# Attention with one key block of six, and the last head's last, multiplied with v in 4-byte operands

## The chip, the cores and the metric

One core of one Trainium2 chip. The metric is the device time of one execution in microseconds: 743.06 us, the median of 3 runs (742.97 to 743.62).

## What is computed

Attention over 4 batches of 8 heads, 768 positions and 64 columns, in which a query sees only keys whose 6 sign bits of a random projection are the same, and behind it a layer of 8 experts. The change touches the attention alone:

```python
q_bits = (np.einsum('bhsd,dk->bhsk', q, proj) > 0); k_bits = ...
mask = q_bucket[:, :, :, None] == k_bucket[:, :, None, :]
scores = np.where(mask, scale * np.matmul(q, k.transpose(0, 1, 3, 2)), -1e9)
scores = scores - np.max(scores, axis=-1, keepdims=True)
attn = np.exp(scores)
attn = attn / (np.sum(attn, axis=-1, keepdims=True) + 1e-09)
return np.matmul(attn, v)
```

The result of attention decides which tokens each expert takes, in order of their logits.

## The kernel before

The work is one program on five engines, whose order is written out by hand. Attention (`attention`, up to about 405 us) takes the 32 heads one after the other, in 8 groups G of 4 heads. A head has 768 keys, which are 6 key blocks `kc` of 128.

A number of 4 bytes is kept as two numbers of 2 bytes, a high part and a low part, and a product is made of products of parts. For v these are `VH` (f16, with a 65th column of ones that gives the row sums) and `VL`, made for each head by `cv` (L186, a cast on ACT) and `sv` (L187, a subtraction).

The loop at the end of `attention` runs over steps t, one key block each, and in a step over the letters of `ORD`, 'SF0r1LRA':

- S: `S_pass` (L230, L232): scores of 128 queries on PE, and DVE's maximum over keys.
- 0 and 1: `ST` (L254 to L256): the transposed scores of block t, 384 queries at a time, in two matmuls on PE, and the exponential on ACT into `pt`, 128 keys by 768 queries of 4 bytes.
- L: `lo` (L259): the low part of `pt`, that is `pt` less its own upper two bytes read as bf16, for the block of the step before. `PAT` gives blocks 0 and 5 of even heads and block 3 of odd ones to DVE, and the rest to POOL; the first two heads have lists of their own, and the last block of all is DVE's.
- F or A: `AV` (L269 to L271): the product of block t-4 (`LAG` is 4) with v, accumulated in PSUM (`psv`). For each of the 6 pieces of 128 queries there are three matmuls, with 128 weight columns of `pt` or `lo` and 64 or 65 moving columns of v:

```python
T.matmul(av[:,c,:],ph[:,r],VH[u][:,j,kc,:],...)
T.matmul(av[:,c,0:64],ph[:,r],VL[u][:,j,kc,:],...)
T.matmul(av[:,c,:],l[:,r],VH[u][:,j,kc,:],...)
```

- r and R: everything with a step number of its own: the casts and subtractions for the next groups, `project` (L142, signs of a later group: 4-byte operands, 32 weight columns, 384 moving ones), `m_rows` (L239, L240), `sumv` (L197 to L200), and after each pair of heads `xtr` (L296 to L298, 4-byte transposes of 128 by 128).

After the last block `norm` divides by the row sums. Behind attention the routing and the 8 experts follow (from L312 on); the change does not touch them.

Of the kernel before, what the change touches and what calls it, by code (L numbers as in the profile page):

```python
# [8 lines left out]
F32 = mybir.dt.float32  # L9
F16 = mybir.dt.float16  # L10
# [3 lines left out]
ALU = mybir.AluOpType  # L14
# [4 lines left out]
AP=dict(PAT=[[0, 5], [3]],  # L19
 ORD='SF0r1LRA',  # L20
 LAG=4,
 E0=[3, 5],
 E1=[3, 4],
 X=[2, 2, 5],
 MR=2,
 LEAD=9,
 S=[7, 30],
# [3 lines left out]
 P3=[69, 73, 82, 80, 84, 86, 89, 86, 75, 83, 87, 90, 94, 96, 97, 99, 2, 3, 115, 58, 62, 87],  # L31
 P4=[-33, -33, -25, -21, -13, -7, -11, -7, -20, -16, -5, -2, -7, 5, 8, 3, 1, 4, 14, -56, -51, -11],
 L0=[89, 4],
 EA=[268, 32, 5],
 MV=[23, 24, 28, 59, 96, 1],
 CL=9,
# [3 lines left out]
PAT,E0,E1,DW,LEAD=(AP[k] for k in ('PAT','E0','E1','DW','LEAD'))  # L40
# [3 lines left out]
def attention(tc, nc, ctx, qT, kT, vv, proj, wg, x_dram, L, jp, identf, B, late=None, after=None):  # L44
    S=768; NG=2*B; NH=8*B; LAG=AP['LAG']
    cp=ctx.enter_context(tc.tile_pool(name="cp",bufs=1))
    dp=ctx.enter_context(tc.tile_pool(name="dp",bufs=2))
# [3 lines left out]
    V=nc.vector; A=nc.scalar; G_=nc.gpsimd; T=nc.tensor; SY=nc.sync  # L51
    BOTH=slice(0,2)

    LD={}
    def alloc_load(G):
        LD[G]=(dp.tile([128,2,S],F32,name="qp",bufs=1),dp.tile([128,2,S],F32,name="kp",bufs=1),dp.tile([128,4,6,64],F32,name="vp",bufs=1))
# [32 lines left out]
    pos=row(96,1.0,"pos"); neg=row(99,-1.0,"neg")  # L89
    kc=cp.tile([128,1],F32,name="kc"); V.scalar_tensor_tensor(kc,c70,-6.0,pos,op0=ALU.mult,op1=ALU.add)  # L90
    V.tensor_tensor(kc,kc,neg,op=ALU.add)
    QA=[];KA=[];QB=[];KB=[];VH=[];VL=[];WF=[]
    for u in range(2):
        for l,n in ((QA,"qa"),(KA,"ka"),(QB,"qb"),(KB,"kb")): l.append(cp.tile([128,4,2*HK if l is KA else S],F16,name=f"{n}{u}"))
    def init(j,eng):
# [18 lines left out]
    for u in range(2):  # L114
        VH.append(cp.tile([128,4,6,65],F16,name=f"vh{u}")); VL.append(cp.tile([128,4,6,64],F16,name=f"vl{u}"))
        G_.memset(VH[u][:,:,:,64:65],1.0)
        WF.append(cp.tile([128,4,65],F16,name=f"wf{u}")); G_.memset(WF[u],0.0)


# [28 lines left out]
    def sides(G):  # L148

        return [(slice(64*hh,64*hh+64),2+hh) for hh in range(2)]  # L150
    def his(G):
        u=G%2; h=TMP[G,'h']
        for qk,(a,b,r0) in enumerate(((QA,QB,0),(KA,KB,64))):
            for r,j in sides(G): SY.dma_start(a[u][0:64,j,0:S],h[qk][r,1])
            for r,j in sides(G): SY.dma_start(b[u][r0:r0+64,j,:],h[qk][r,1])
    def dbits(G):
        u=G%2; bt=TMP[G,'b']
        for hh in range(2):
            for w,dst in enumerate((QA,KA)): SY.dma_start(dst[u][64:70,2+hh,0:S],bt[64+32*w+6*hh:70+32*w+6*hh,:])
    def lows(G):  # L160
        u=G%2; l=TMP[G,'l']
        for r,j in sides(G): SY.dma_start(KB[u][0:64,j,:],l[1][r,1]); SY.dma_start(QB[u][64:128,j,:],l[0][r,1])
    def moves(G,part=0):


        u=G%2; h=TMP[G,'h']; l=TMP[G,'l']; bt=TMP[G,'b']
        hs=[(slice(64*hh,64*hh+64),slice(hh,4,2)) for hh in range(2)]
        def go(dst,src,r0=0):
            for r,js in hs: SY.dma_start(dst[u][r0:r0+64,js,0:S],src[r])
        def signs_():  # L170
            for j in range(4):
                for w,dst in enumerate((QA,KA)):
                    a=64*(j//2)+32*w+6*(j%2)
                    SY.dma_start(dst[u][64:70,j,0:S],bt[a:a+6,:])
        def nxt(w):
            if G+1<NG: load(G+1,w)
        if part==1: todo=(go,QA,h[0]),(go,KA,h[1]),(signs_,)
        elif part==2: todo=(go,QB,h[0]),(nxt,0),(go,KB,h[1],64),(nxt,1)
        elif part==3: todo=()
        else: todo=(go,QA,h[0]),(go,QB,h[0]),(nxt,0),(go,KA,h[1]),(go,KB,h[1],64),(signs_,),(nxt,1)  # L180
        for f,*x in todo: f(*x)
        if part in (0,3): go(KB,l[1]); go(QB,l[0],64)
    def clear(G):

        SY.dma_start(QA[G%2][96:128].rearrange("p j (z q) -> p (j z) q",z=2),wrm[0:32,None,0:384].to_broadcast([32,8,384]))
    def cv(G,j): A.copy(VH[G%2][:,j,:,0:64],LD[G][2][:,j])  # L186
    def sv(G,j,e=None): (e or V).tensor_tensor(VL[G%2][:,j],LD[G][2][:,j],VH[G%2][:,j,:,0:64],op=ALU.subtract)  # L187
    def sumv(G):
        u=G%2
        if G<2:  # L190
            V.tensor_copy(WF[u][96:128,:,64],wc[96:128,:].to_broadcast([32,4]))
        ps=psT.tile([128,512],F32,name="pst")
        pv=ps[96:128,0:256].rearrange("p (j d) -> p j d",j=4)
        n=0
        for c in range(6):
            for src in (VH[u],VL[u]):
                T.matmul(ps[:,0:256].rearrange("p (j d) -> p j d",j=4),on,src[:,:,c,0:64],start=n==0,stop=n==11,skip_group_check=True); n+=1  # L197
        hi=dp.tile([128,4,64],F16,name="shi",bufs=1)
        A.copy(hi[96:128],pv)
        V.scalar_tensor_tensor(WF[u][96:128,:,0:64],hi[96:128],ml[96:128],pv,op0=ALU.mult,op1=ALU.add)  # L200
# [20 lines left out]
        else: G_.tensor_tensor(QB[0][64:128,j],qd[64:128,j],QB[0][64:128,j],op=ALU.subtract)  # L221


    M6={}
    def S_pass(h,qc):
        G,j=divmod(h,4); u=G%2
        if qc==0: M6[h]=dp.tile([128,6],F16,name="m6",bufs=3)
        ps=psS.tile([128,2,512],F32,name="pss")
        for hf in range(2):
            T.matmul(ps[:,hf,0:HK],QA[u][:,j,qc*128:qc*128+128],KA[u][:,j,hf*HK:hf*HK+HK],start=True,stop=True)  # L230
            if h==0: warm(DW[1],DW[4])
        V.tensor_reduce(M6[h][:,qc:qc+1],ps[:,:,0:HK],axis=AX.XY,op=ALU.max,negate=True)  # L232
    MR={}
    def m_rows(h,hf):
        G,j=divmod(h,4)
        if h>=2:
            ps=psS.tile([128,2,512],F32,name="pss")
            for c in range(6):
                T.matmul(ps[:,c//3,c%3*128:c%3*128+128],M6[h][:,c:c+1].to_broadcast([128,128]),ident,start=True,stop=True)  # L239
            A.activation(QA[G%2][96:128,j,:].rearrange("p (z q) -> p z q",z=2),ps[96:128,:,0:384],AF.Relu,bias=mbi[96:128],scale=msc[96:128])  # L240
            return
        MR[hf]=psT.tile([128,512],F32,name="pst")
        for c in range(3):
            T.matmul(MR[hf][:,c*128:c*128+128],M6[h][:,3*hf+c:3*hf+c+1].to_broadcast([128,128]),ident,start=True,stop=True)
        A.activation(QA[G%2][96:128,j,hf*384:hf*384+384],MR[hf][96:128,0:384],AF.Relu,bias=mbi[96:128],scale=msc[96:128])


    PT={}
    def ST(h,kc,hf):
        G,j=divmod(h,4); u=G%2  # L250
        if hf==0: PT[h,kc]=(dp.tile([128,S],F32,name="pt",bufs=7),dp.tile([128,S],F16,name="lo",bufs=7))
        ps=psT.tile([128,512],F32,name="pst")
        r=slice(hf*384,hf*384+384); kr=slice(kc*128,kc*128+128)
        T.matmul(ps[:,0:384],KA[u][:,j,kr],QA[u][:,j,r],start=True,stop=False)  # L254
        T.matmul(ps[:,0:384],KB[u][:,j,kr],QB[u][:,j,r],start=False,stop=True)  # L255
        A.activation(PT[h,kc][0][:,r],ps[:,0:384],AF.Exp,scale=0.125)  # L256
    def lo(h,kc,eng):
        p,l=PT[h,kc]
        eng.tensor_tensor(l,p,p.bitcast(BF)[:,1::2],op=ALU.subtract)  # L259
    AVt={}  # L260
    def AV(h,kc):
        G,j=divmod(h,4); u=G%2
        if kc==0: AVt[h]=psV.tile([128,512],F32,name="psv")
        av=AVt[h][:,0:390].rearrange("p (c d) -> p c d",c=6)
        p,l=PT[h,kc]
        ph=p.bitcast(BF)[:,1::2]
        for c in range(6):
            r=slice(c*128,c*128+128)
            T.matmul(av[:,c,:],ph[:,r],VH[u][:,j,kc,:],start=(kc==0 and c==0),stop=False,skip_group_check=True)  # L269
            T.matmul(av[:,c,0:64],ph[:,r],VL[u][:,j,kc,:],start=False,stop=False,skip_group_check=True)  # L270
            T.matmul(av[:,c,:],l[:,r],VH[u][:,j,kc,:],start=False,stop=False,skip_group_check=True)  # L271
        if kc==5:
            for c in range(6):

                if j==3: T.matmul(av[:,c,:],QA[u][96:128,j,c*128:c*128+128],WF[u][96:128,j,:],start=False,stop=(c==5),skip_group_check=True,tile_position=(96,0))
                else: T.matmul(av[:,c,:],QA[u][:,j,c*128:c*128+128],WF[u][:,j,:],start=False,stop=(c==5),skip_group_check=True)
# [90 lines left out]
    def step(o,t):  # L367
        h,s=divmod(t,6)
        first=(t-LAG)%6==5
        if o=='F' and first or o=='A' and not first: av(t)  # L370
        elif o=='0' and t<6*NH and t not in early: ST(h,s,0)
        elif o=='1' and h<NH: ST(h,s,1)
        elif o=='S':
            for x in S_at.get(t,[]): S_pass(*x)
        elif o in 'rR': run(2*t+(o=='R'))
        elif o=='L' and t>=1 and (t-1)//6<NH:
            hh,ss=divmod(t-1,6)
            lo(hh,ss,V if ss in (E0 if hh<1 else E1 if hh<2 else PAT[hh%len(PAT)]) or t==6*NH else G_)
    for t in range(6*NH+LAG+6):
        for o in AP['ORD']: step(o,t)  # L380

# [532 lines left out]
```

## Time and profile before

| | |
|---|---|
| median of 3 runs | 743.06 us |
| the profiled execution's own time | 740.94 us |
| its span in the profile | 739.1 us |
| busy in the span: PE, DVE, POOL, ACT | 670.2, 557.2, 527.6, 393.5 us |
| attention | to about 405 us |
| low parts (L259) | 144 on POOL, 48 on DVE |
| products with v (L269 to L271) | 3 x 1152 matmuls |

Busy time is the union of an engine's instructions. A matmul's record lasts from its start until its last column is out, so matmuls that follow each other overlap in the rows, and the distance of their starts tells what each takes. PEld is TensorE's loading of weights, which can run under a matmul. A wait is named by the instruction that waited and by the one whose end released it.

### The profile page before, as it was taken

How to read it: one execution, taken by the hardware profiler on the slowest of the kernel's cores; microseconds unless marked ns; L12 is line 12 of the kernel's file. 1: busy time of each engine (PE TensorE's matmuls, PEld its weight loads, DVE VectorE, ACT ScalarE, POOL GpSimd, SP SyncE). 2: the span in 40 equal slices, each digit the busy share in tenths (PEclk: the TensorE clock that was granted, in tenths of full speed). 3: DMA queues.
4: the chain of work that ended last, by engine and by line, in shares of the span. 5: the costliest groups of instructions: out<-in, count | busy, mean ns of one | idle time of the engine just before them, and what ended most of it. 6: DMA issues, size and time to landing. Idle time of an engine off the chain costs nothing. (4 is left out here: it accounts for less than half of the span.)

```text
span 739.1 us, 19123 instructions
## 1 busy us (share of the span) xinstructions
PE 670.2 (91%) x7735; PEld 435.1 (59%) x7748; DVE 557.2 (75%) x1315; ACT 393.5 (53%) x788; POOL 527.6 (71%) x475
## 2 busy tenths in 40 slices
PE   8898888998999989998889568979999999899995
PEld 2565665666777667676667454445555555555552
DVE  7888977888988889989775678887888788853120
ACT  6876575676776766655556034433544444444430
POOL 7895949597795977855556077695969597978751
PEclk9999999999999999999999569999999999999998
DMA  8638664525447254440000061707071707171701
GB/s 215 196 85 201 155 160 115 138 66 133 120 123 192 70 132 121 122 111 22 6 19 24 24 219 53 281 33 270 31 282 42 272 34 284 45 270 57 272 28 44
DMA packets 40002, 93.59 MB, mean 127 GB/s; under 512 B 4597, under 2 KB 30569, under 8 KB 37865
## 3 DMA queue, kind: packets, MB, share of 16 engines
q1 hardware_dynamic: 33048, 46.21, 24.4%
q0 software_dynamic: 6784, 46.14, 17.5%
q8 instruction: 61, 1.00, 0.6%
q14 instruction: 29, 0.23, 0.1%
q10 hardware_dynamic: 80, 0.00, 0.0%
HBM read 59.53 MB, written 12.58 MB: 98 GB/s over the span
## 5 line engine op out<-in xcount | busy, mean ns | idle before, releaser
L259 POOL TENSOR_TENSOR lo<-pt 128x768 f16<-128x768 f32 x144 | 227.8, 1594 | 83.8 <-ACT pt L256 81.9
L256 ACT ACTIVATE pt<-pst 128x384 f32<-128x384 f32 x384 | 174.7, 491 | 118.1 <-PE pst L255 105.0
L232 DVE TENSOR_REDUCE m<-pss 128x1 f16<-128x770 f32 x192 | 181.0, 955 | 29.8 <-PE pss L230 28.2
L254 PE MATMUL pst<-qa,ka 128*128 128x384 f16 x384 | 125.2, 326 | 9.1 <-ACT pt L256 6.1
L271 PE MATMUL psv<-vh,lo 128*128 128x65 f16 x1152 | 124.3, 194 | 4.1 <-POOL lo L259 4.1
L255 PE MATMUL pst<-qb,kb 128*128 128x384 f16 x384 | 125.3, 326 | 1.8 <-DMA qb<-ql 1.8
L270 PE MATMUL psv<-vl,pt 128*128 128x64 f16 x1152 | 124.9, 193 | 0.6 <-issue 0.6
L269 PE MATMUL psv<-vh,pt 128*128 128x65 f16 x1152 | 124.7, 195 | 0.0
L269 PEld LDWEIGHTS <-pt 128*128 128x128 bf16 x1152 | 107.4, 98 | 15.0 <-issue 3.3
L270 PEld LDWEIGHTS <-pt 128*128 128x128 bf16 x1152 | 106.2, 99 | 12.1 <-issue 0.9
L271 PEld LDWEIGHTS <-lo 128*128 128x128 f16 x1152 | 106.2, 98 | 4.7 <-POOL lo L259 4.6
L230 PE MATMUL pss<-ka,qa 128*128 128x385 f16 x384 | 94.6, 328 | 11.7 <-DVE m L232 8.3
L751 POOL TENSOR_TENSOR wl<-wf,wh 128x512 bf16<-128x512 f32 x90 | 101.7, 1147 | 0.3 <-ACT wh L739 0.3
L739 ACT CAST wh<-wf 128x1024 f16<-128x1024 f32 x64 | 65.4, 1040 | 39.3 <-DMA wf<-in_w_dram,zwidx 39.2
L787 ACT ACTIVATE hh<-ph 128x384 f16<-128x384 f32 x64 | 31.4, 490 | 79.4 <-PE ph L785 79.4
L785 PEld LDWEIGHTS <-wh 128*128 128x128 f16 x512 | 49.0, 97 | 35.1 <-issue 4.3
L259 DVE TENSOR_TENSOR lo<-pt 128x768 f16<-128x768 f32 x48 | 62.7, 1307 | 3.1 <-ACT pt L256 2.5
L788 DVE SCALAR_TENSOR_TENSOR hl<-ph,hh 128x384 f16<-128x384 f32 x64 | 34.8, 553 | 34.2 <-ACT hh L787 33.6
L797 PEld LDWEIGHTS <-hh 128*128 128x128 f16 x384 | 36.1, 97 | 37.4
L255 PEld LDWEIGHTS <-kb 128*128 128x128 f16 x384 | 37.4, 97 | 30.9 <-issue 11.7
L785 PE MATMUL ph<-xh,wh 128*128 128x384 f16 x256 | 53.5, 326 | 1.9 <-DVE hl L788 1.6
L785 PE MATMUL ph<-xl,wh 128*128 128x384 f16 x256 | 52.9, 326 | 0.0
(265 smaller groups left out, 1255.8 us busy)
## 6 DMA issues: line engine op xcount, KB each, us to landing
vp<-in_vv_dram SPq DMA_DIRECT2D x8, 768.0 KB
x_dram<-X SPq DMA_DIRECT2D x16, 384.0 KB
qp<-in_qT_dram SPq DMA_DIRECT2D x7, 768.0 KB
kp<-in_kT_dram SPq DMA_DIRECT2D x7, 768.0 KB
qa<-qh SPq DMA_DIRECT2D x14, 192.0 KB
ka<-kh SPq DMA_DIRECT2D x14, 192.0 KB
qb<-qh SPq DMA_DIRECT2D x14, 192.0 KB
kb<-kh SPq DMA_DIRECT2D x14, 192.0 KB
```

Of the source, the lines that this page charges most:

```text
L230: T.matmul(ps[:,hf,0:HK],QA[u][:,j,qc*128:qc*128+128],KA[u][:,j,hf*HK:hf*HK+HK],start=True,stop=True)
L232: V.tensor_reduce(M6[h][:,qc:qc+1],ps[:,:,0:HK],axis=AX.XY,op=ALU.max,negate=True)
L254: T.matmul(ps[:,0:384],KA[u][:,j,kr],QA[u][:,j,r],start=True,stop=False)
L255: T.matmul(ps[:,0:384],KB[u][:,j,kr],QB[u][:,j,r],start=False,stop=True)
L256: A.activation(PT[h,kc][0][:,r],ps[:,0:384],AF.Exp,scale=0.125)
L259: eng.tensor_tensor(l,p,p.bitcast(BF)[:,1::2],op=ALU.subtract)
L269: T.matmul(av[:,c,:],ph[:,r],VH[u][:,j,kc,:],start=(kc==0 and c==0),stop=False,skip_group_check=True)
L270: T.matmul(av[:,c,0:64],ph[:,r],VL[u][:,j,kc,:],start=False,stop=False,skip_group_check=True)
L271: T.matmul(av[:,c,:],l[:,r],VH[u][:,j,kc,:],start=False,stop=False,skip_group_check=True)
L739: s.nc.scalar.copy(h[:,r],f[:,r])
L751: for _ in range(n): s.nc.gpsimd.tensor_tensor(*s.pend.pop(0)[1],op=ALU.subtract)
L785: T.matmul(p[:,0:384],a[:,o:o+128],b[:,d],start=n==0,stop=n==11)
```

## The change

`FK` names the key blocks that are multiplied whole: block 2 of every head, and blocks 2 and 5 of the last head, 33 blocks in all. For them there is no low part of `pt` (`lo` isn't called, and the pool of low parts has 6 buffers instead of 7), and `AV` has 6 matmuls of 4-byte operands in place of 18: `pt` as it is, against `VF`, v in 4 bytes with a column of ones. `VF` is filled by a copy on ACT behind each cast of v, and its ones by two memsets on POOL at the start. The functions `wrote` and `holds` and the tables `KEEP`, `passes` and `maxed` issue no instruction: they raise an error while the program is written if a table would read something out of turn.

```diff
+ FK=[[2],[2,5]],
...
+    FS=sorted({kc for l in AP['FK'] for kc in l})
+    def whole(h): return AP['FK'][h==NH-1]
...
+        VF.append(cp.tile([128,4,len(FS),65],F32,name=f"vf{u}")); G_.memset(VF[u][:,:,:,64:65],1.0)
...
-    def cv(G,j): A.copy(VH[G%2][:,j,:,0:64],LD[G][2][:,j])
+    def cv(G,j):
+        A.copy(VH[G%2][:,j,:,0:64],LD[G][2][:,j]); wrote(f'vh{j}',G)
+        for i,kc in enumerate(FS):
+            if kc in whole(4*G+j): A.copy(VF[G%2][:,j,i,0:64],LD[G][2][:,j,kc])
...
-        if hf==0: PT[h,kc]=(dp.tile([128,S],F32,name="pt",bufs=7),dp.tile([128,S],F16,name="lo",bufs=7))
+        if hf==0: PT[h,kc]=(dp.tile([128,S],F32,name="pt",bufs=7),None if kc in whole(h) else dp.tile([128,S],F16,name="lo",bufs=6))
...
-        for c in range(6):
+        if kc in whole(h):
+            for c in range(6):
+                T.matmul(av[:,c,:],p[:,c*128:c*128+128],VF[u][:,j,FS.index(kc),:],start=(kc==0 and c==0),stop=False,skip_group_check=True)
+        else:
+          for c in range(6):
...
-            lo(hh,ss,V if ss in (E0 if hh<1 else E1 if hh<2 else PAT[hh%len(PAT)]) or t==6*NH else G_)
+            if ss not in whole(hh): lo(hh,ss,V if ss in (E0 if hh<1 else E1 if hh<2 else PAT[hh%len(PAT)]) or t==6*NH else G_)
```

On PE, block 2 of a head in the middle stands between the second half of a step's scores (`pst`) and the next pass for the maxima (`pss`). Before, its first piece of queries was (five more of the same kind follow):

```order
L255 LDWEIGHTS kb_173
L255 MATMUL pst<-qb_172,kb_173 128x384
L269 LDWEIGHTS pt
L269 MATMUL psv<-vh_204,pt 128x65
L270 LDWEIGHTS pt
L270 MATMUL psv<-vl_205,pt 128x64
L271 LDWEIGHTS lo
L271 MATMUL psv<-vh_204,lo 128x65
```

With the change the whole block is one row, six instructions that carry their own weights, with no load written out:

```order
L283 LDWEIGHTS kb_173
L283 MATMUL pst<-qb_172,kb_173 128x384
L301 MATMUL psv<-vf_207,pt 128x65 x6
L253 LDWEIGHTS qa_170
L253 MATMUL pss<-ka_171,qa_170 128x385
```

Eighteen pairs of load and matmul became six 4-byte matmuls in the same place; line numbers are those of the changed file, and everything else on PE stands in its order.

On POOL, low parts stand among the subtractions for the next group's q and k (`ql`, `kl`). Before, in the second group:

```order
L259 TENSOR_TENSOR lo<-pt 128x768 x2
L128 TENSOR_TENSOR ql<-qp,qh 128x768
L259 TENSOR_TENSOR lo<-pt 128x768 x3
L128 TENSOR_TENSOR ql<-qp,qh 128x768
L259 TENSOR_TENSOR lo<-pt 128x768
L128 TENSOR_TENSOR kl<-kp,kh 128x768
L259 TENSOR_TENSOR lo<-pt 128x768
```

With the change:

```order
L287 TENSOR_TENSOR lo<-pt 128x768 x2
L137 TENSOR_TENSOR ql<-qp,qh 128x768
L287 TENSOR_TENSOR lo<-pt 128x768 x2
L137 TENSOR_TENSOR ql<-qp,qh 128x768
L287 TENSOR_TENSOR lo<-pt 128x768
L137 TENSOR_TENSOR kl<-kp,kh 128x768
L287 TENSOR_TENSOR lo<-pt 128x768
```

A run of three became two where a block 2 stood in it, and nothing else moved; over the program 32 go from POOL and one from DVE.

## Rows read from the trace of the kernel before

**Rows 1.** The page of the profile, part 2: the whole span in 40 equal slices of 18.5 us, busy share of PE and clock granted to TensorE, each digit in tenths.

```profile
PE   8898888998999989998889568979999999899995
...
PEclk9999999999999999999999569999999999999998
```

**Rows 2.** Busy time by window, all of attention after its start-up: from and to, length, then busy us of PE, its weight loads, DVE, ACT and POOL with instructions in brackets, granted clock, share of DMA, GB/s.

```profile
20.00:405.00 385.00, 354.23 (x5399) 258.65 (x5397) 324.70 (x444) 255.37 (x556) 283.46 (x208) 1.00 0.43 111
```

**Rows 3.** The same view of two stretches of 11 us in the middle of attention.

```profile
185.00:196.00 11.00, 11.00 (x170) 8.46 (x169) 10.50 (x15) 8.37 (x19) 6.00 (x6) 1.00 0.82 201
...
207.00:218.00 11.00, 11.00 (x173) 7.50 (x172) 9.70 (x14) 7.65 (x18) 10.62 (x8) 1.00 0.13 36
```

**Rows 4.** Waits of PE from 20 to 405 us, by what ended them: total us, times, longest us.

```profile
PE pss L230 <- DVE m L232: 7.5, 11, 1.2
PE pst L254 <- ACT pt L256: 6.1, 8, 0.9
PE psv L271 <- POOL lo L259: 4.1, 4, 2.2
PE pss L230 <- ACT qa L240: 2.6, 3, 1.0
PE pss L239 <- DVE m L232: 2.2, 2, 1.9
PE pst L254 <- DVE XT L298: 2.1, 3, 1.1
...
PE pst L305 <- DVE XT L298: 0.8, 2, 0.4
PE pst L296 <- DVE X L286: 0.7, 4, 0.2
```

**Rows 5.** The page, part 5: line, engine, operation, what it writes and reads, shapes, count, then busy us and mean ns of one, then idle us of the engine before them and what ended it.

```profile
L259 POOL TENSOR_TENSOR lo<-pt 128x768 f16<-128x768 f32 x144 | 227.8, 1594 | 83.8 <-ACT pt L256 81.9
L256 ACT ACTIVATE pt<-pst 128x384 f32<-128x384 f32 x384 | 174.7, 491 | 118.1 <-PE pst L255 105.0
...
L254 PE MATMUL pst<-qa,ka 128*128 128x384 f16 x384 | 125.2, 326 | 9.1 <-ACT pt L256 6.1
...
L259 DVE TENSOR_TENSOR lo<-pt 128x768 f16<-128x768 f32 x48 | 62.7, 1307 | 3.1 <-ACT pt L256 2.5
```

**Rows 6.** Line 259, the low parts of the exponentials: durations min/median/max in ns, first and last start in us.

```profile
L259 POOL TENSOR_TENSOR lo<-pt x144: 1459/1467/2237, 24.3 to 403.2; 128x768 f16<-128x768 f32 x144
...
L259 DVE TENSOR_TENSOR lo<-pt x48: 941/959/2265, 27.2 to 404.4; 128x768 f16<-128x768 f32 x48
```

**Rows 7.** Timeline of DVE where the last head ends: start us, duration us, line and operation, and in brackets the idle time before it and what ended it.

```profile
404.43 1.10 DVE L259 TENSOR_TENSOR lo<-pt 128x768 f16<-128x768 f32 x1 [1.03 <-ACT pt L256]
```

**Rows 8.** Groups of ACT by line, shapes kept apart, columns as in rows 5: the copies nearest to the new ones in size.

```profile
L464 ACT ACTIVATE tb<-iof 128x64 bf16<-128x64 f32 x5 | 1.3, 261 | 0.0
...
L439 ACT COPY dm<-dm 128x32 f32<-128x32 f32 x1 | 0.2, 218 | 0.0
```

**Rows 9.** Timeline of PE through one block's product with v, its first four matmuls and its last, and the matmul that follows it: start us, duration us, line, operation.

```profile
200.01 0.19 PE L269 MATMUL psv<-vh,pt 128*128 128x65 f16 x1
200.04 0.19 PE L270 MATMUL psv<-vl,pt 128*128 128x64 f16 x1
200.06 0.20 PE L271 MATMUL psv<-vh,lo 128*128 128x65 f16 x1
200.09 0.20 PE L269 MATMUL psv<-vh,pt 128*128 128x65 f16 x1
...
200.52 0.19 PE L271 MATMUL psv<-vh,lo 128*128 128x65 f16 x1
200.55 0.19 PE L276 MATMUL psv<-wf,qa 128*128 128x65 f16 x1
```

**Rows 10.** Lines 142 (the projection) and 296 (the transposes), loads and matmuls: durations min/median/max in ns, first and last start, forms. The projection's later groups write pss.

```profile
L142 PEld LDWEIGHTS pss<-qp,pr x56: 106/110/111, 41.1 to 303.4; 128*32 128x32 f32 x56
L142 PE MATMUL pss<-qp,pr x56: 486/486/511, 41.1 to 303.7; 128*32 128x384 f32 x56
...
L296 PEld LDWEIGHTS pst<-identf,X x96: 137/141/231, 51.6 to 408.1; 128*128 128x128 f32 x96
L296 PE MATMUL pst<-identf,X x96: 272/273/421, 51.7 to 408.2; 128*128 128x128 f32 x96
```

**Rows 11.** Timeline of the projection's first pair of instructions (qp and kp, two passes each), loads first, then matmuls.

```profile
12.56 0.11 PEld L142 LDWEIGHTS pst<-qp,pr 128*32 128x32 f32 x1 [0.62 <-issue]
12.57 0.11 PEld L142 LDWEIGHTS pst<-kp,pr 128*32 128x32 f32 x1
12.59 0.11 PEld L142 LDWEIGHTS pst<-qp,pr 128*32 128x32 f32 x1
12.60 0.11 PEld L142 LDWEIGHTS pst<-kp,pr 128*32 128x32 f32 x1
...
12.57 0.51 PE L142 MATMUL pst<-qp,pr 128*32 128x384 f32 x1
...
12.91 0.49 PE L142 MATMUL pst<-qp,pr 128*32 128x384 f32 x1
```

**Rows 12.** Timeline of transposes that stand first after a pause, loads and matmuls (x2 merges two loads into one row, from the first's start to the second's end).

```profile
202.74 0.14 PEld L296 LDWEIGHTS pst<-identf,X 128*128 128x128 f32 x1 [0.52 <-issue]
202.77 0.30 PE L296 MATMUL pst<-identf,X 128*128 128x128 f32 x1 [0.16 <-DVE X L286]
...
407.57 0.20 PEld L296 LDWEIGHTS pst<-identf,X 128*128 128x128 f32 x2 [1.00 <-DVE X L286]
407.58 0.33 PE L296 MATMUL pst<-identf,X 128*128 128x128 f32 x1 [0.88 <-DVE X L286]
```

**Rows 13.** Timeline of PE at 343 us, one row.

```profile
343.42 0.49 PE L239 MATMUL pss<-ident,m 128*128 128x128 f16 x6 [1.92 <-DVE m L232]
```

**Rows 14.** Busy time by window after it, columns as in rows 2.

```profile
344.00:348.00 4.00, 3.96 (x31) 2.65 (x30) 3.48 (x7) 2.89 (x5) 1.90 (x2) 0.57 0.32 98
348.00:352.00 4.00, 4.00 (x67) 3.11 (x66) 3.37 (x6) 2.24 (x5) 1.31 (x2) 1.00 0.02 4
```

More of the change, by code (lines that the diff above doesn't have):

```diff
@@ L52, in attention, with wrote, holds @@
     BOTH=slice(0,2)
+    FS=sorted({kc for l in AP['FK'] for kc in l})
+    def whole(h): return AP['FK'][h==NH-1]
+    KEEP={}
+    def wrote(w,G): KEEP[w,G%2]=KEEP.get((w,G%2),[])+[G]
+    def holds(G,**need):
+        for w,n in need.items():
+            if KEEP.get((w,G%2),[])[-n:]!=[G]*n: raise ValueError(f'{w} of group {G} is read out of turn')
     LD={}
@@ L91, in attention @@
     V.tensor_tensor(kc,kc,neg,op=ALU.add)
-    QA=[];KA=[];QB=[];KB=[];VH=[];VL=[];WF=[]
+    QA=[];KA=[];QB=[];KB=[];VH=[];VL=[];VF=[];WF=[]
     for u in range(2):
@@ L154, in his @@
             for r,j in sides(G): SY.dma_start(a[u][0:64,j,0:S],h[qk][r,1])
+            wrote('hi',G)
             for r,j in sides(G): SY.dma_start(b[u][r0:r0+64,j,:],h[qk][r,1])
@@ L159, in dbits @@
             for w,dst in enumerate((QA,KA)): SY.dma_start(dst[u][64:70,2+hh,0:S],bt[64+32*w+6*hh:70+32*w+6*hh,:])
+        wrote('sign',G)
     def lows(G):
@@ L162, in lows @@
         for r,j in sides(G): SY.dma_start(KB[u][0:64,j,:],l[1][r,1]); SY.dma_start(QB[u][64:128,j,:],l[0][r,1])
+        wrote('low',G)
     def moves(G,part=0):
@@ L169, in go @@
             for r,js in hs: SY.dma_start(dst[u][r0:r0+64,js,0:S],src[r])
+            wrote('hi' if dst in (QA,KA) else 'low',G)
         def signs_():
@@ L174, in signs_ @@
                     SY.dma_start(dst[u][64:70,j,0:S],bt[a:a+6,:])
+            wrote('sign',G)
         def nxt(w):
@@ L183, in clear, with sv @@
     def clear(G):
+        wrote('clear',G)
         SY.dma_start(QA[G%2][96:128].rearrange("p j (z q) -> p (j z) q",z=2),wrm[0:32,None,0:384].to_broadcast([32,8,384]))
-    def cv(G,j): A.copy(VH[G%2][:,j,:,0:64],LD[G][2][:,j])
-    def sv(G,j,e=None): (e or V).tensor_tensor(VL[G%2][:,j],LD[G][2][:,j],VH[G%2][:,j,:,0:64],op=ALU.subtract)
+    def cv(G,j):
+        A.copy(VH[G%2][:,j,:,0:64],LD[G][2][:,j]); wrote(f'vh{j}',G)
+        for i,kc in enumerate(FS):
+            if kc in whole(4*G+j): A.copy(VF[G%2][:,j,i,0:64],LD[G][2][:,j,kc])
+    def sv(G,j,e=None):
+        holds(G,**{f'vh{j}':1}); wrote(f'vl{j}',G)
+        (e or V).tensor_tensor(VL[G%2][:,j],LD[G][2][:,j],VH[G%2][:,j,:,0:64],op=ALU.subtract)
     def sumv(G):
-        u=G%2
+        u=G%2; holds(G,vh0=1,vh1=1,vh2=1,vh3=1,vl0=1,vl1=1,vl2=1,vl3=1); wrote('wf',G)
         if G<2:
@@ L221, in rlo @@
         else: G_.tensor_tensor(QB[0][64:128,j],qd[64:128,j],QB[0][64:128,j],op=ALU.subtract)
-    M6={}
+    M6={}; passes={}; maxed=[]
     def S_pass(h,qc):
         G,j=divmod(h,4); u=G%2
+        if G: holds(G,hi=2,sign=1)
+        if G>1: holds(G,clear=1)
+        passes[h]=passes.get(h,0)+1
         if qc==0: M6[h]=dp.tile([128,6],F16,name="m6",bufs=3)
@@ L235, in m_rows @@
         G,j=divmod(h,4)
+        if passes[h]<(6 if h>=2 else 3*hf+3): raise ValueError('a maximum is not whole')
+        maxed.extend([(h,0),(h,1)] if h>=2 else [(h,hf)])
         if h>=2:
@@ L250, in ST @@
         G,j=divmod(h,4); u=G%2
-        if hf==0: PT[h,kc]=(dp.tile([128,S],F32,name="pt",bufs=7),dp.tile([128,S],F16,name="lo",bufs=7))
+        if (h,hf) not in maxed: raise ValueError('a head has no maximum')
+        if G: holds(G,hi=2,sign=1)
+        if G: holds(G,low=1)
+        if hf==0: PT[h,kc]=(dp.tile([128,S],F32,name="pt",bufs=7),None if kc in whole(h) else dp.tile([128,S],F16,name="lo",bufs=6))
         ps=psT.tile([128,512],F32,name="pst")
@@ L262, in AV @@
         G,j=divmod(h,4); u=G%2
+        holds(G,**{f'vh{j}':1,f'vl{j}':1})
+        if kc==5:
+            holds(G,wf=1)
+            if KEEP.get(('clear',G%2),[G])[-1]!=G: raise ValueError('maxima are cleared too soon')
         if kc==0: AVt[h]=psV.tile([128,512],F32,name="psv")
```

## The prediction

> **What bounds the kernel now.** The clock came first, because a price read at one clock doesn't hold at the other: TensorE has its full clock (1.0, the 2.4 GHz level) through nearly all of attention, which runs to about 405 us [rows 1]. Then the totals of that stretch: from 20 to 405 us PE is busy 354 of 385 us, DVE 325, POOL 283, ACT 255 [rows 2]. A busy PE isn't a full PE, so next I looked at single heads in the middle. In 185:196 and 207:218, eleven microseconds each, about one of the 32 heads, PE is busy all the time, while DVE has about 10 us, POOL 6.0 and 10.6 and ACT about 8 [rows 3]. The reader should see that a head's period is there the length of PE's own list of matmuls. Last, what PE still waits for: over all of attention DVE's maxima 7.5 and 2.2 us, ACT's exponentials 6.1 us, POOL's low parts 4.1 us in 4 waits [rows 4]. So POOL's largest group, 144 low parts and 228 us [rows 5], is nearly all beside the path. POOL waits for ACT rather than being waited for.
>
> **What goes away.** Of 192 low parts 33 go: key block 2 of each of the 32 heads, always POOL's, and block 5 of the last head, DVE's. POOL loses 32 x 1594 ns = 51 us [rows 5]. What the path can get of that is the 4.1 us that PE waits for it [rows 4]; nearly all, as POOL loses 51 of its 283 us [rows 2]: -4 us. There is a second way. POOL's low part takes 1467 ns at the median and up to 2237, DVE's 959 and up to 2265 [rows 6]: the long ones are where the two run together, 63 us for DVE's 48 [rows 5] where 959 ns each would be 46. With 32 of 144 POOL pieces gone, some 22% of those 17 us, about 4, come off DVE. The last head's block 5 frees DVE of 1.10 us between its exponential and its product, with PE's block behind it [rows 7]: -1 us.
>
> **What comes in beside the path.** ACT gets 33 copies of 128x64 4-byte elements, between 218 ns (128x32) and 261 ns (128x64 with a scale) by the nearest rows [rows 8]: 33 x 0.25 = 8 us. They stand behind a cast of v; ACT idles 105 us before exponentials waiting for PE [rows 5]: cost nothing, and at most their 8 us if that idle time went. Two memsets on POOL before the first product and one buffer fewer for low parts (six hold them where five of six blocks use one): nothing, as AV runs four blocks behind.
>
> **What comes in on the path.** A block now is 18 matmuls. In the timeline they start 30 ns apart, from 200.01 to the next group's start at 200.55 us: 0.54 us [rows 9]. Their weight loads don't show: each hides under the matmul before it.
> After, a block is six 4-byte instructions with 128 weight columns and 65 moving ones. No row shows that shape, so I bound it by the two 4-byte kinds that there are.
> First, the count. The projection (line 142) is a true 4-byte product: 7 groups x 2 halves x 2 pairs = 28 instructions with qp, but 56 loads and 56 matmuls in the trace [rows 10]. So each gives two passes, and a block 12 loads and 12 matmuls.
> Second, the streaming. A matmul of 384 columns takes 486 ns as 4-byte, 326 as 2-byte (line 254) [rows 10, 5], so 160 ns more for 384 columns: 0.83 ns a column instead of 0.42. 65 columns are 54 ns a pass.
> Third, the load, on which all hangs. In the projection the first matmul of a pair starts with its load but takes 0.51 us instead of 0.49, and the second load of the same columns (qp) starts at 12.59 after 12.56 [rows 10, 11]: the first matmul, 510 against 486 ns, was held by 24 ns, and with the 2 ns or so that its start lies behind the load, 32 columns cost some 26 ns, 0.81 ns a column. In the 4-byte transposes (line 296), which give one matmul an instruction (96 for 96), 128 columns cost less: the first matmul takes 0.30 where 273 ns is usual, and starts at 202.77 behind a load of 202.74, so streaming began 57 ns after the load; the two loads at 407.57 take 0.20 in all with 0.14 for one, 0.06 apart [rows 10, 12].
> So the ends: at the transposes' rate 57 ns a load, at the product's 4 x 26 = 104 ns. Loads run one ahead, under the matmul before: the projection's second pair of loads starts while the first pair of matmuls streams [rows 11]. A pass then lasts as long as the longer of load and stream, with 2 to 3 ns between: 60 or 107 ns, a block 0.72 or 1.28 us. I take 107: line 142 is the same kind of instruction, with both passes, and the transposes are another. Extra on PE: 33 x (1.28 - 0.54) = +24.4 us; at the cheap end 33 x (0.72 - 0.54) = +6 us. If loads weren't hidden at all, 12 x (104 + 54) = 1.90 us and +45 us.
> The Trainium skill's page "TensorE: Matmul & The Clock Gate", section "LDWEIGHTS (loading the stationary operand)", gives a load as its columns over 1.2 GHz, which is 107 ns for 128 columns; the sum would be 33 x (12 x 0.110 - 0.54) = +25.7 us by it, against +6 by the transposes. By that rule 32 columns are 26.7 ns, and line 142 agrees (26); the transposes' 57 ns do not. The same page, section "Weight-path perf modes", keeps the fast load to operands that aren't FP32, which speaks against this change.
>
> **What of the 24.4 is given back.** The heads in [rows 3] have no slack: there +0.74 us a head stays. Elsewhere PE waits for DVE 7.5 + 2.2 + 2.1 us [rows 4]; a PE that is later, and a DVE that POOL lengthens less, shorten these. I take half: -6 us. ACT's 6.1 us I leave, since ACT works on what PE has just given it. One of DVE's waits, 1.92 us before 343.42, is followed by a stretch at a mean clock of 0.57 of 1.0, 4 us long [rows 13, 14]: 0.43 x 4 = 1.7 us that would return with that wait gone; an even chance: -1 us.
> **Sum:** 24.4 - 4 - 1 - 6 - 1 = +12.4 us. Against the profiled execution, 740.94 us (span 739.1, the rest around it unchanged), that is 753.3; the median of the runs is 2.1 us above it, so 743.06 + 12.4 = **755.5 us**. What follows attention keeps its work and only starts later. With 18 of the 26 us of waits in [rows 4] gone (POOL's 4 among them) it is 24.4 - 18 - 2, about +5; with none of DVE's, half of POOL's and no change of clock 24.4 - 2 - 1 = +21: 748 to 764.
>
> **Rivals.**
> *Cheap loads.* 4-byte weights of 128 columns load as in the transposes: +6 on PE, -4 for POOL's waits, -1 at the end, -3 for DVE (PE is hardly later, so mostly the port of 4 us) and -1 for the clock: -3 us, 740; 736 to 744. For it: the transposes have this element size and these 128 columns, and a fixed 16 ns with 0.32 ns a column would fit both kinds of load. Against: 0.32 ns is less than a cycle at the full clock (0.42), and line 142's columns cost two cycles in its matmuls too. This is the side on which the kernel gets faster; it decides below a pass of about 70 ns, where 33 blocks cost the 10 us or so that come back.
> *Slow loads, absorbed.* DVE, not PE, sets the pace in most heads (325 of 385 us busy), and of its 22 us of waits for others than POOL [rows 4] 17 turn into room: 24.4 - 17 - 4, about +3, 746. Against: the middle heads of [rows 3] have no PE idle time at all.
> *Loads not hidden.* Each 4-byte pass waits for its own load: +45 - 12 = +33, 776. For it: a load that takes longer than the stream before it is seen nowhere. Against: the projection's loads go in early.
>
> **How the numbers follow.** Slow loads mostly on the path 0.65 (755.5), cheap loads 0.24 (740), absorbed 0.08 (746), not hidden 0.03 (776). The range 739 to 764 leaves out the lower half of the cheap case (about 0.09), the top of the likeliest and the last: 0.17 or so. The likeliest's own range is 748 to 764. Within 0.2%, about 1.5 us, is what a measurement can't tell from no change. Faster by more: 0.17 of the cheap case and 0.01 of the absorbed, 0.18. Same: 0.06. Slower: 0.76.
>
> **What would show it.** The 4-byte product with line and tile psv<-vf,pt: 396 loads and 396 matmuls; starts 107 ns apart within a block and a block of 1.28 us (60 ns and 0.72 in the cheap case). Heads in the middle 11.7 us apart instead of about 11.0, attention's last product some 12 us later, POOL's group at 112 pieces, no wait of PE for POOL's low parts, DVE's low parts at a lower mean than 1307 ns. Wrong if starts are about 60 ns apart, or if the starts are as said but the middle heads keep their 11 us.

## The result and the profile after

The kernel with the change takes 754.84 us, median of 4 runs (752.51 to 755.14), against 743.34 us before: ratio 1.0145 with a 95% interval of 1.0121 to 1.0169, so slower by 11.5 us by the medians and by 10.8 by the ratio. 755.5 was predicted. The profiled execution took 755.06 us, with a span of 753.3 us. Three single executions among all runs took 1122 us (the kernel before), 2140 us (the first profiled one of the run without low parts) and 2371 us (the run with the first 12 heads), and the ratios leave them out.

The page of the changed kernel, parts 1 and 5 (columns as in [rows 5]; line 287 is the low part, 284 the exponential):

```profile
PE 695.1 (92%) x7537; PEld 462.0 (61%) x7550; DVE 547.0 (73%) x1314; ACT 398.2 (53%) x821; POOL 476.7 (63%) x445
...
L287 POOL TENSOR_TENSOR lo<-pt 128x768 f16<-128x768 f32 x112 | 174.6, 1566 | 140.4 <-ACT pt L284 139.8
L284 ACT ACTIVATE pt<-pst 128x384 f32<-128x384 f32 x384 | 174.1, 491 | 125.6 <-PE pst L283 118.2
...
L287 DVE TENSOR_TENSOR lo<-pt 128x768 f16<-128x768 f32 x47 | 58.3, 1241 | 2.1 <-ACT pt L284 1.6
```

POOL has its 112 low parts, at 1566 ns instead of 1594, DVE 47 at 1241 instead of 1307 [rows 5]. So some 47 x 66 ns = 3 us came off DVE, where about 4 were expected. ACT waits longer for PE, 118 us instead of 105: everything now stands more behind PE than before.

The new product, line 301, by line with durations min/median/max in ns:

```profile
L301 PEld LDWEIGHTS psv<-vf,pt x396: 187/192/193, 30.7 to 416.7; 128*128 128x128 f32 x198
L301 PE MATMUL psv<-vf,pt x396: 218/275/303, 30.8 to 416.7; 128*128 128x65 f32 x198
```

396 loads and 396 matmuls for 198 instructions: two passes each. The timeline of one block in the middle and of the matmul that follows it (start us, duration us; 12 records are merged into one row, from the first's start to the last's end):

```profile
194.51 0.33 PE L283 MATMUL pst<-qb,kb 128*128 128x384 f16 x1
194.67 1.45 PE L301 MATMUL psv<-vf,pt 128*128 128x65 f32 x12
195.96 0.49 PE L253 MATMUL pss<-ka,qa 128*128 128x385 f16 x2
```

From 194.67 to the next group's start at 195.96 is 1.29 us, where [rows 9] had 0.54. Inside the block the passes start 0.11 us apart, but for the first two (56 ns): the first load went in under the matmul before the block. So the block is eleven loads of 111 to 112 ns and one last stream of 56. Under each matmul lies the load of the next pass, whose record is 192 ns long.

Busy time by window, columns as in [rows 2]: a stretch in the middle, all of attention, and 4 us at 332 us:

```profile
190.00:201.75 11.75, 11.75 (x164) 9.10 (x163) 9.59 (x16) 8.19 (x17) 8.30 (x7) 1.00 0.32 79
...
20.00:417.70 397.70, 378.67 (x5249) 286.22 (x5248) 315.43 (x445) 259.49 (x588) 232.60 (x176) 1.00 0.42 107
...
332.00:336.00 4.00, 4.00 (x26) 2.67 (x25) 0.99 (x2) 0.84 (x2) 0.00 (x0) 0.58 0.04 10
```

The first stretch was chosen 11.0 + 0.75 us long, and PE is busy in all of it, as it was in the 11.0 us of [rows 3]. That shows no idle time there, but not how long a head is; the reciprocals below show that. Over attention PE is idle for 397.7 - 378.7 = 19.0 us; before it was 31 (385 - 354 to 405 us [rows 2]). So the waits gave back some 12 us. Which ones, the waits of PE tell (total us, times, longest us), to be read beside [rows 4]:

```profile
PE pst L282 <- ACT pt L284: 8.7, 12, 1.2
PE pss L253 <- ACT qa L265: 2.6, 3, 1.0
PE pss L253 <- DVE m L255: 2.4, 5, 1.1
PE psv L307 <- POOL lo L287: 1.4, 1, 1.4
PE pst L341 <- DVE XT L334: 0.8, 2, 0.4
PE pst L282 <- DVE XT L334: 0.5, 1, 0.5
...
PE pst L269 <- DVE m L255: 0.3, 1, 0.3
```

The waits for POOL's low parts went from 4.1 to 1.4 us, those for DVE's maxima from 9.7 to 2.7. Those for ACT's exponentials grew from 6.1 to 8.7.

Where the time went in the end: the reciprocal of a head's row sums is DVE's first long step after its product, one a head. In the changed kernel those of heads 6 and 7 and of the last two start at

```profile
115.00 0.19 DVE L320 RECIPROCAL r<-r 128x6 f32<-128x6 f32 x1
...
126.93 0.19 DVE L320 RECIPROCAL r<-r 128x6 f32<-128x6 f32 x1
...
410.22 0.19 DVE L320 RECIPROCAL r<-r 128x6 f32<-128x6 f32 x1
417.51 0.19 DVE L320 RECIPROCAL r<-r 128x6 f32<-128x6 f32 x1
```

and in the first profile of the kernel before at

```profile
115.39 0.19 DVE L284 RECIPROCAL r<-r 128x6 f32<-128x6 f32 x1
...
129.62 0.19 DVE L284 RECIPROCAL r<-r 128x6 f32<-128x6 f32 x1
...
401.27 0.19 DVE L284 RECIPROCAL r<-r 128x6 f32<-128x6 f32 x1
406.94 0.19 DVE L284 RECIPROCAL r<-r 128x6 f32<-128x6 f32 x1
```

The last one starts at 417.51. In the first profile of the kernel before it started at 406.94, in a second one (below) at 405.97. The difference is 10.6 or 11.5 us, all of it inside attention. The profiles' spans differ by 14.2 us, but 3.6 of these lie behind attention, where nothing was changed, and the second profile of the kernel before has them too (741.7 - 406.0 = 335.7 us behind the last reciprocal; 753.3 - 417.5 = 335.8 with the change, 332.2 in the first profile). From head 7 to head 30 a head takes 12.3 us on average, (410.22 - 126.93) / 23, where it took 11.8, (401.27 - 129.62) / 23: of a block's 0.74 us some 0.5 stays.

### The profile page after: what moved, and what is told of

Its sections match the earlier page's. It is cut to its first block, busy times and chain, and to the rows that moved or that the text cites. A ratio compares the mean times of both kernels' runs of the same rounds, so it can differ in the third digit from the quotient of the medians.

```text
span 753.3 us, 18703 instructions
## 1 busy us (share of the span) xinstructions
PE 695.1 (92%) x7537; PEld 462.0 (61%) x7550; DVE 547.0 (73%) x1314; ACT 398.2 (53%) x821; POOL 476.7 (63%) x445
## 5 line engine op out<-in xcount | busy, mean ns | idle before, releaser
L287 POOL TENSOR_TENSOR lo<-pt 128x768 f16<-128x768 f32 x112 | 174.6, 1566 | 140.4 <-ACT pt L284 139.8
L307 PE MATMUL psv<-vh,lo 128*128 128x65 f16 x954 | 102.8, 194 | 1.4 <-POOL lo L287 1.4
L306 PE MATMUL psv<-vl,pt 128*128 128x64 f16 x954 | 102.9, 193 | 0.0
L305 PE MATMUL psv<-vh,pt 128*128 128x65 f16 x954 | 102.8, 194 | 0.0
L305 PEld LDWEIGHTS <-pt 128*128 128x128 bf16 x954 | 88.8, 98 | 13.0 <-issue 3.1
L306 PEld LDWEIGHTS <-pt 128*128 128x128 bf16 x954 | 87.7, 99 | 9.5
L307 PEld LDWEIGHTS <-lo 128*128 128x128 f16 x954 | 87.8, 97 | 1.5 <-POOL lo L287 1.5
L287 DVE TENSOR_TENSOR lo<-pt 128x768 f16<-128x768 f32 x47 | 58.3, 1241 | 2.1 <-ACT pt L284 1.6
```

## Experiments

The theory: a pass lasts as long as its weight load, 107 to 112 ns, that price falls on PE's list of matmuls, and the missing low parts give back a part of it through the waits for POOL and DVE. The rivals: streaming or a fixed price sets the pass; low parts are beside the path altogether; every block costs the same wherever it stands.

**Is it the load? 64 weight columns instead of 128.**

```diff
-T.matmul(av[:,c,:],p[:,c*128:c*128+128],VF[...],...)
+T.matmul(av[0:64,c,:],p[:,c*128:c*128+64],VF[...],...)
```

> The change with 64 instead of 128 weight columns in the 4-byte matmuls (the other half of the queries gets nothing of those blocks). Streaming stays 65 columns, 12 passes a block. Theory (a pass lasts as long as its load, 0.83 ns a column with 128 columns hidden under nothing): a load falls to about 54 ns, the pass to the streaming time, 57 to 60 ns, a block to 0.70 us; the time falls by most of 33 x 0.58 = 19 us, to 738 to 743, where the case of cheap loads lay. Rival (a pass is limited by streaming or by a fixed price per 4-byte matmul): passes stay at 111 ns, time 753 to 756.

Measured: 744.03 us, ratio 1.0016 to the kernel before (0.9998 to 1.0035). Line 301 by line, durations min/median/max in ns:

```profile
L301 PEld LDWEIGHTS psv<-vf,pt x396: 132/138/138, 35.5 to 408.3; 128*64 128x64 f32 x198
L301 PE MATMUL psv<-vf,pt x396: 222/222/272, 35.5 to 408.3; 128*64 128x65 f32 x198
```

and one block in the timeline:

```profile
206.38 0.91 PE L301 MATMUL psv<-vf,pt 128*64 128x65 f32 x12
```

Twelve passes end within 0.91 us of the first's start instead of 1.45, and the starts inside a block are 58 to 59 ns apart. That is near the streaming time (56 ns) and near half of the load's 112, and this run can't tell which of the two sets it; the next run helps. The block is 0.85 us to the next group's start, not 0.70: its first two starts are 107 ns apart and the next group starts 0.15 us after the last, neither of which was expected, and so the time lies 1 us above the range given. At half the load the price of the blocks, 33 x (0.85 - 0.54) = 10 us, is about what the waits give back, and the kernel stands where it stood before the change. The rival is out.

**Is it the streaming? 32 moving columns instead of 65.**

```diff
-T.matmul(av[:,c,:],p[...],VF[u][:,j,FS.index(kc),:],...)
+T.matmul(av[:,c,33:65],p[...],VF[u][:,j,FS.index(kc),33:65],...)
```

> The change with 32 instead of 65 moving columns of v in the 4-byte matmuls (the other columns get nothing of those blocks), weights as they are. Theory (a pass lasts as long as its load): passes stay at 111 ns, blocks at 1.28 us, time within 1.5 us of the change, 753 to 756. Rival (streaming, 27 instead of 54 ns, is part of the pass beside the load): passes fall to about 84 ns, blocks to 1.0 us, and the time by up to 9 us, to 746.

Measured: 752.45 us, ratio 1.0137 (1.0114 to 1.0159), a median 2.4 us under the change with intervals that overlap. Line 301, durations as above:

```profile
L301 PEld LDWEIGHTS psv<-vf,pt x396: 187/192/192, 30.3 to 414.5; 128*128 128x128 f32 x198
L301 PE MATMUL psv<-vf,pt x396: 191/276/276, 30.5 to 414.6; 128*128 128x32 f32 x198
```

One block in the timeline:

```profile
204.80 1.42 PE L301 MATMUL psv<-vf,pt 128*128 128x32 f32 x12
```

Half the columns, and the block has kept its length but for the last pass: 1.42 us from the first start to the last end instead of 1.45, 1.26 to the next group instead of 1.29. Starts stay 111 to 112 ns apart, but for the first two (28 ns instead of 56), so streaming lies under the load in all passes but the last. That one is 28 ns shorter, 33 x 28 ns = 0.9 us; the time is 0.6 us below what was expected. Halving the load's columns shortened the passes by half and halving the stream's did not, so the load sets them.

**What do the blocks cost with the low parts still made?**

```diff
-if ss not in whole(hh): lo(...)
+lo(...)
```

> The change, but the low parts of the whole blocks are still computed (33 more, read by nobody; 7 buffers again), so only TensorE's side and the copies of the change are left. Theory (the 4-byte passes cost the path 33 x 0.745 = 24.6 us, part of it absorbed by waits, and the missing low parts give back some 8 us): 760 to 765 us, slower than the change by 5 to 10. Rival 1 (low parts are beside the path, and waits alone absorb the difference): within 2 us of the change, 753 to 757. Rival 2 (nothing is absorbed): 767 or more.

Measured: 760.84 us, ratio 1.0236 to the kernel before (1.0196 to 1.0275): 17.5 us. The sum of the blocks is 33 x (1.285 - 0.54) = 24.6, so waits take up about 7 even without any relief, and the relief is worth about 6 more (760.84 against 754.84). Two waits of PE in its profile:

```profile
PE pss L253 <- DVE m L255: 7.2, 11, 1.1
PE psv L307 <- POOL lo L287: 2.1, 2, 1.1
```

With the low parts made, PE still waits 7.2 us for DVE's maxima in line 253, where [rows 4] had 7.5; without them 2.4. Both rivals are out: the low parts are not beside the path, and the blocks' price is not paid in full.

**What are the low parts worth alone?** The edit is against the change; the copies of v and their tile are left out with it, and the pool of low parts keeps its 6 buffers.

```diff
-T.matmul(av[:,c,:],p[...],VF[...],...)
+T.matmul(av[:,c,:],ph[:,r],VH[u][:,j,kc,:],...)
+T.matmul(av[:,c,0:64],ph[:,r],VL[u][:,j,kc,:],...)
+T.matmul(av[:,c,:],ph[:,r],VH[u][:,j,kc,:],...)
```

> The kernel before, but the low parts of the same 33 blocks are not computed; their product still has its 18 two-byte matmuls, with the high part in the place of the low part, and there are no 4-byte copies of v. So only the relief of POOL and DVE is left; the low parts' share of the output is missing. Theory: 743.3 - 6 to 10 us, that is 733 to 737: the 4 us of PE's waits for POOL, part of its 12 us of waits for DVE, and 1 us at the end. Rival 1 (low parts are beside the path): 741 to 744. With e1 and the change: if relief and price simply add, this run less the kernel before is the change less e1.

Measured: 735.08 us, ratio 0.9895 (0.9863 to 0.9927), 7.8 us faster. With the 17.5 of the last run that makes +9.7, against +10.8 for the change by its ratio: price and relief add, within the intervals. For its profile the same program ran once more:

> The same program as e2_no_low_18, for a profile: the product of the 33 blocks has 18 two-byte matmuls without low parts of the exponentials. Theory: PE's waits for POOL's low parts near zero, its waits for DVE's maxima less than half of 9.7 us, attention's last product 6 to 10 us before the 407 us of the kernel before. Rival (low parts are beside the path): waits and end as before.

Its one time was 734.73 us, and waits of PE in attention were

```profile
PE pss L250 <- DVE m L252: 5.0, 7, 2.1
PE psv L307 <- POOL lo L284: 1.9, 3, 1.5
PE pss L261 <- DVE m L252: 0.9, 2, 0.6
```

The waits for POOL fell from 4.1 to 1.9, where near zero was expected, those for DVE's maxima from 9.7 to 5.9, where under half was expected: both less than expected. The last reciprocal starts about 10 us before that of the first profile, as far as was expected.

**Does the last block of the last head pay?**

```diff
- FK=[[2],[2,5]],
+ FK=[[],[5]],
```

> The change for one block alone, the last head's last; all others as before. Theory: DVE's 1.10 us between the last exponential and its product goes, the block costs 0.75 us more, with one block of matmuls of the head queued ahead: -1 to +1 us, 742 to 744. Rival (the end of attention waits for the low part and for nothing else): -1.1 us or a little more at once, under 742.

Measured: 738.78 us, ratio 0.9971 (0.9937 to 1.0006), which doesn't tell the two apart. The profile does. The reciprocals of the last two heads:

```profile
396.08 0.19 DVE L320 RECIPROCAL r<-r 128x6 f32<-128x6 f32 x1
402.55 0.19 DVE L320 RECIPROCAL r<-r 128x6 f32<-128x6 f32 x1
```

The last head takes 6.47 us after the one before it; in the kernel before it took 5.67 (401.27 to 406.94). So the block cost 0.8 us, its whole price, and the 1.10 us of DVE [rows 7] gave nothing back: PE was still multiplying the blocks queued ahead when the low part was ready (in the kernel before it ended at 405.53 us, and PE multiplied blocks without a pause from 404.43 to 406.35). That the median is 2.8 us under the kernel before comes, by the profile, from other heads: head 30 ends 4 to 5 us earlier here (396.08) than in the two profiles of the kernel before (401.27, and 400.33 below), although no block up to there is whole. So some of what differs in time between such programs isn't the blocks; this run serves as the comparison for the last one below.

**Does a block cost the same in every head?** Head by head against the first profile, the changed kernel was 2.3 us ahead at the end of head 11 and lost 0.6 us a head from there. Three runs put the whole blocks elsewhere:

```diff
-def whole(h): return AP['FK'][h==NH-1]
+def whole(h): return [2] if h<12 else []
...
+def whole(h): return [] if h<12 else AP['FK'][h==NH-1]
...
+def whole(h): return [2] if h in (2,3,6,7) else []
```

> Block 2 whole in the first 12 heads alone, the rest as before. Theory (the price falls on the path only where TensorE has no waits; head by head the change was 2.3 us ahead at the end of head 11 and lost 0.6 us a head from there): 739.5 to 742.5, a gain of 1 to 3 us on the kernel before. Rival (the price of a block is the same in all heads): 12/33 of the change's 11.5 us, that is 747.

> The complement: block 2 whole in heads 12 to 31 and block 5 in the last, the first 12 heads as before. Theory: the loss of the change and what the first heads had given back, 743 + 11.5 + 2.3 = 755 to 759. Rival (same price in all heads): 21/33 of 11.5 us, that is 750.

> Block 2 whole in heads 2, 3, 6 and 7 alone, those before the two places where the change was ahead by 1.7 and 2.3 us at one blow. Theory (it is the backlog of POOL and DVE there that the missing low parts end): 739 to 741.5, as good as or better than with the first 12. Rival (the gain needs all of the 12): 742.5 or more.

Measured: the first 12 heads 741.46 us, ratio 0.9986 (0.9956 to 1.0017); from head 12 on 750.89, ratio 1.0146 (1.0096 to 1.0195); four heads 739.77, ratio 0.9981 (0.995 to 1.0011). The first 12 cost nothing that the times show, where equal prices would have made it 4 us: that rival is out. It stays out when 1.6 us are set aside that this run gains at heads 17 and 28, which have no whole block in it (see the last run): its interval then ends at 2.9. The second run's interval, 7 to 14.5 us, holds both of its cases, and the four heads' holds no gain as well as 3.7 us: by the times these two are inconclusive.

The profiles showed a mistake in the reading. In the run from head 12 on, head 3 ended 3 us early although no block is whole there. So the 1.7 us of the change in head 3 can't be put down to its whole blocks: the first profile of the kernel before has this wait of PE there (at 70 us), which not every profile has:

```profile
PE pst L255 <- DMA qb<-ql: 1.8, 1, 1.8
```

To see how much is one execution's own, the kernel before ran once more, for one time of 743.52 us and a profile:

> The kernel before, unchanged, for a second profile. If heads 3 and 25 to 28 of the first profile were one execution's own (a DMA that landed late, a stretch at the lower clock), this one ends attention 2 to 5 us earlier than that one's 407 us; if they are the program's, within 0.5 us of it.

Its reciprocals of heads 6 and 7 and of the last two:

```profile
115.31 0.19 DVE L284 RECIPROCAL r<-r 128x6 f32<-128x6 f32 x1
...
130.68 0.19 DVE L284 RECIPROCAL r<-r 128x6 f32<-128x6 f32 x1
...
400.33 0.19 DVE L284 RECIPROCAL r<-r 128x6 f32<-128x6 f32 x1
405.97 0.19 DVE L284 RECIPROCAL r<-r 128x6 f32<-128x6 f32 x1
```

Attention ends 1.0 us earlier than in the first profile, which is neither of the two cases. The wait for the DMA is there again, at 69 us, so of head 3 it can't be said that it was one execution's own:

```profile
PE pst L255 <- DMA qb<-ql: 1.7, 1, 1.7
```

What was one execution's own is the place of the stretch at the lower clock. In the first profile it lies at 344 us [rows 14], and head 26 takes 11.8 us there; in the second head 26 takes 10.7, and the stretch comes at 124 us, behind a wait for POOL's low part. The row of PE that waited, and busy time by window behind it (columns as in [rows 2]):

```profile
123.92 0.20 PE L271 MATMUL psv<-vh,lo 128*128 128x65 f16 x1 [2.21 <-POOL lo L259]
```

```profile
124.00:128.00 4.00, 4.00 (x43) 2.67 (x44) 1.82 (x2) 1.49 (x3) 3.92 (x3) 0.57 0.97 239
```

So head 7 takes 15.4 us in the second profile (115.31 to 130.68) and 14.2 in the first, and the 1.2 us between them are about what the stretch costs at head 26. With the change head 7 takes 11.9, and the wait of 2.2 us at 124 us, which both profiles of the kernel before have, is gone. That gain at head 7 is the change's.

**The version that this points to: heads 6 and 7 alone** (`h in (6,7)`).

> Block 2 whole in heads 6 and 7 alone. Theory (what is worth having of the missing low parts is the backlog on POOL that ends in a wait of 2 us near 124 us; the gain in head 3 was another execution's DMA wait and not the change): 1 to 3 us faster than the kernel before, no worse than with four or twelve heads. Rival (the few us by which such kernels were ahead come from elsewhere): within 1 us of the kernel before.

Measured: 737.63 us, ratio 0.994 (0.9911 to 0.9968): 4.4 us faster than the kernel before (2.4 to 6.6), and the lowest median here of those that compute all of the attention, though its interval overlaps those of the runs with four heads and with the last block alone. Its reciprocals and three of its waits:

```profile
114.44 0.19 DVE L320 RECIPROCAL r<-r 128x6 f32<-128x6 f32 x1
...
126.36 0.19 DVE L320 RECIPROCAL r<-r 128x6 f32<-128x6 f32 x1
...
395.68 0.19 DVE L320 RECIPROCAL r<-r 128x6 f32<-128x6 f32 x1
401.32 0.19 DVE L320 RECIPROCAL r<-r 128x6 f32<-128x6 f32 x1
```

```profile
PE pss L253 <- DVE m L255: 6.7, 11, 1.2
PE pst L282 <- ACT pt L284: 6.5, 9, 0.9
PE psv L307 <- POOL lo L287: 1.3, 1, 1.3
```

Head 7 takes 11.9 us, and the waits for POOL are 1.3 us where the second profile of the kernel before has 4.4. Two blocks' price, 1.5 us, buys the end of POOL's backlog, which is where the next group's subtractions stand between the low parts.

But the 4.4 us are not all the two blocks'. The stretch at the lower clock is back behind DVE's wait, as in the first profile of the kernel before, so what head 7 no longer pays for it, head 26 pays (11.8 us):

```profile
340.00:344.00 4.00, 4.00 (x31) 2.69 (x31) 3.12 (x6) 2.58 (x5) 2.27 (x2) 0.57 0.32 98
```

Heads 6, 7 and 8 together take 38.7 us here and 41.3 and 42.2 in the two profiles of the kernel before; with 1.2 us of the stretch taken off the 42.2, the two blocks gain 2.3 to 2.6 us there, their price paid. The runs from head 12 on and with the last block alone, which leave these heads as they were, take 40.8 and 41.8 with the stretch in them (39.6 and 40.6 without), which makes it 0.9 to 2.0. Another 1.3 us is gained at head 28 and 0.3 at head 17, where no block is whole; at head 28 this wait of the kernel before is gone:

```profile
374.35 0.32 PE L230 MATMUL pss<-ka,qa 128*128 128x385 f16 x1 [1.12 <-DVE m L232]
```

The run with the last block alone has these two gains as well, and its head 30 ends at 396.08 us, only 0.4 us behind this one's 395.68. They therefore don't come from heads 6 and 7. Against the kernel before, both programs have six buffers for low parts instead of seven and the tile for v in 4 bytes; which of these does it, if either, was not tried.

## Why the prediction was right

- **The load.** The step on which all hung held: 4 x 26 = 104 ns was predicted from 32 columns, 107 for a pass, and a pass takes 111 to 112; a block takes 1.285 us where 1.28 was said. That the two agree so closely is luck: said were twelve passes of 107 ns, measured are eleven of 111 to 112 and a last stream of 56. The price on PE is 24.6 us (24.4 said). Halving the weights nearly halved the pass, halving the stream did not. The 4-byte transposes were the wrong neighbours for it, as was assumed. The Trainium skill's page "TensorE: Matmul & The Clock Gate", section "LDWEIGHTS (loading the stationary operand)", gives a load as its columns over 1.2 GHz, for 128 columns an estimate of 107 ns; for the 4-byte product the trace agrees (111 to 112 ns a pass), for the 4-byte transposes it doesn't [rows 12].
- **No slack in the middle**, +0.74 us a head said: from head 7 to head 30 a head went from 11.8 to 12.3 us, so 0.5 stayed. The windows of 11 us that were read as heads are full of PE's work, but they are not heads: single heads take between 9 and 15 us, and about a third of a block's price comes back on average there too.
- **POOL's waits**, -4 said: 4.1 to 1.4, so -2.7. Mis-sized, since one wait stayed.
- **DVE's waits**, -6 said: 7.5 + 2.2 + 2.1 became 2.4 + 0.3 + 0.5, so about -8.6. With the low parts kept, 7.2 us of the 7.5 stayed, so there it was the relief rather than PE's delay that ended them; the 2.2 and the 2.1 fell to 0.3 and 0.6 in that run, so those PE's delay had ended.
- **ACT's waits**, 0 said: 6.1 to 8.7 us. This was missed: PE waits more often for the exponentials. The copies of v, put at nothing, do a part of it: at 179, 227, 277 and 325 us one or two of them (0.25 us each) stand on ACT ahead of the activation for the maxima (L265), and PE's wait behind it is 1.06 to 1.21 us, where four such waits before were 0.92 each; that is 0.7 us in all. Three new waits of 0.52 us (at 203, 252 and 300 us) have no copy ahead of them, and what brings them was not tried.
- **The end**, -1 said: nothing came back; the block cost its 0.8 us.
- **The clock**, -1 said at an even chance: a stretch at the lower level is there again, 0.58 of full over 4 us at 332 us, with PE busy all of it. Nothing came back: the wait of 1.92 us is gone, but the stretch then came elsewhere, at head 24, where the last wait of more than 1 us before it is one of 1.21 for ACT at 325 us.
- **Sum.** 12 us were to come back, and 31 - 19 = 12 us less idle time is what PE shows. But the terms inside missed by up to 3 us each and with both signs, and the waits that had a term gave back only 2.7 + 8.6 - 2.6 = 8.7. Most of the rest came from waits that had none: the 1.8 us for the DMA at 70 us and 1.0 for POOL's subtraction of v (L197), both absent with the change. That the total is 1 us off is luck in part.

## What to carry to other kernels

A 4-byte product whose moving side is narrow is bound by its weight loads: here 65 moving columns against 128 weight columns cost 111 ns a pass and 1.285 us a block, where eighteen 2-byte matmuls took 0.54. Price it by the row of the nearest instruction that does the same thing (a true 4-byte product, however small), not by the nearest shape. And a trade of one engine's work for another's is worth making only in those heads whose waits it ends: at heads 6 to 8 two blocks gained 1 to 2.6 us over their price by the profiles, and in all 32 heads the change cost 11.5. When such a version comes out faster, set it against a program that has all of the change but the trade itself: of the 4.4 us here, at least 1.6 were in such a program too.

## What the runs showed of the hardware

The load of a 4-byte product took twice as long per column (192 ns a record for 128 columns, 138 for 64: 0.84 ns a column) as that of a 4-byte transpose (57 ns for 128 columns in all, an estimate from [rows 10, 12], so 0.45 ns a column), though both load 128 columns of 4 bytes. The records of the loads agree: 32 columns have 110 ns [rows 10], 64 have 138 and 128 have 192, which is 84 ns and 0.84 a column; a transpose's load has 141 [rows 10], so 0.45 a column if the 84 are the same there.
